# Decayed linear attention and a soft mixture of experts: late weights loaded into nine buffers that attention leaves, four key turns left out, another order of the first loads and of attention's last steps

## The chip, the cores and the metric

One core of a Trainium2 chip. The metric is the device time of one execution in microseconds (us). All data are float32. TensorE (PE) multiplies, VectorE (DVE), ScalarE (ACT) and GpSimd (POOL) do the elementwise work, and every DMA of the program is issued by SyncE (SP), in the order in which the program names them.

## The reference

Attention runs over 4 batches, 8 heads, 768 positions and 64 channels with one decay `lam` for each head. A block's output is its masked scores times its values plus its decayed queries times the state that earlier blocks left:

```python
intra = np.einsum('bhic,bhjc->bhij', qb, kb) * Dmask[None]
intra = np.einsum('bhij,bhjd->bhid', intra, vb)
inter = np.einsum('bhid,bhde->bhie', qb * lam_pow[None], kv_state)
out[:, :, sl] = intra + inter
...
kv_state = lam_block[None, :, None, None] * kv_state + np.einsum('bhsd,bhse->bhde', kb_dec, vb)
```

The result is taken as 3072 tokens `x` of 512 numbers and goes through a soft mixture of 8 experts with 4 slots each: `logits = x @ phi`; a softmax over the tokens gives the inputs of the 32 slots; every expert does `relu(slot @ w1[e]) @ w2[e]` (512 to 1024 to 512); a softmax over the slots mixes their outputs back into every token. `w1` and `w2` have 16.8 MB each, `q`, `k`, `v` and the output 6.3 MB each.

## The kernel before, in words

The sequence is cut into 24 chunks of 128 positions, and the kernel works on twelve pairs `p` of chunks, the same chunk `n` of two batches. Pairs 0 to 5 are chunks 0 to 5 of batches 0 and 1, pairs 6 to 11 those of batches 2 and 3. The instructions of each engine run in program order (`InOrder`, line 36).

**One pair in the loop** (line 410). `carried` multiplies state and scaled queries, `values` adds masked scores times values in the PSUM banks `xb`, ACT copies the result to `XT`, and `state` (not in the last chunk of a batch) multiplies decayed keys and values; DVE adds that to the state. Then PE does the next pair's `scores`, which DVE masks into `at`, and turns: `turn_k` transposes the next pair's keys, of which DVE makes the decayed keys `kd`; `turn_x` transposes this pair's result, and ACT copies it to `X`. `kd` is read by `state` alone, which pairs 5 and 11 do not run, though their keys are turned. Every second pair does `logits`, and `slots` and `gather` add an earlier group to the slots' running sum `acc`.

**The loads.** A pair's `q`, `k` and `v` (512 KB each) are issued two pairs ahead, each kept behind a PE step of the current pair (`next_load`, line 390 and on). `next_weights` issues one 512 KB tile of `w1`, up to three a pair, into the 32 buffers of the pool `slab`; they are full after pair 9. `w2` has 32 tiles of 512 KB (`load_late`). Five go where pairs 10 and 11 no longer load `q`, `k` and `v`, two into `kd` and `qs` after the loop (lines 467, 468), and 25 into slabs, whose `w1` must have been used first by `first(0)` or `first(1)`.

**The start** (lines 129 to 156): `k` of pair 0, the decays `lam`, then `q` and `v`, each as one DMA for both chunks. DVE makes the mask of eight scans once `lam` is there. `turn_k` of pair 0 uses the banks that `values(0)` needs next (line 406).

**After the loop** (lines 470 to 512): the last group's `logits`, `slots` of the group before it, the maxima, `turn_x` of pair 11, four transposes of stored logits, the exponentials `e`, their transpose `d`, two more transposes, the last slot sums, and a transpose on DVE whose result `sT` is what the experts read. Then come `first(0)` and `first(1)` (the `w1` of experts 0 to 3 and 4 to 7), a long elementwise stretch on DVE, ACT and POOL that makes the mixing weights in the layouts `CR` and `ct`, and `second(0)` and `second(1)` (the `w2`). `second(0)` completes the left half of the experts' outputs; twelve outputs of 256 KB (`put`) of this half are given between the products of `second(1)`, and twelve of the right half after it. A bank of `put` is copied by ACT and DVE in turn and sent by SP.

Of the kernel before, what the change touches and what calls it, by code (L numbers as in the profile page):

```python
# [8 lines left out]
F32 = mybir.dt.float32  # L9
F32R = mybir.dt.float32r  # L10
AF = mybir.ActivationFunctionType
ALU = mybir.AluOpType
AX = mybir.AxisListType

P = 128
B, H, S, DH = 4, 8, 768, 64
# [34 lines left out]
def decay_attn_soft_moe(  # L51
# [30 lines left out]
    def chunk(p, x):  # L82
        b, n = PAIR[p]
        return (b + x) * NB + n
# [7 lines left out]
    def load_in(p, which):  # L92
        for x in which:
            tl = loads.tile([P, 2, 512], F32, tag=x, name=x)
            b, n = PAIR[p]
            src = {"q": qT, "k": kT, "v": vN}[x].rearrange("(b n) p c -> n p b c", n=NB)
            go = sp.dma_start(out=tl, in_=src[n, :, b:b + 2])
            IN[x, p] = tl
        return go
# [20 lines left out]
    def load_late(pool_=None, tag="slab", bufs=None):  # L120
        Q, f, i = late.pop()
        kw = {} if bufs is None else {"bufs": bufs}
        t_ = (pool_ or slabs).tile([P, 2, 512], F32, tag=tag, name="w2t", **kw)
        go = sp.dma_start(out=t_, in_=w2[4 * Q + 2 * i:4 * Q + 2 * i + 2, f].rearrange("e p d -> p e d"))
        for y in range(2):
            wt["w2", Q, 2 * i + y, f] = t_[:, y, :]
        return go

    load_in(0, "k")
    sp.dma_start(out=lam_sb, in_=lam)  # L130
    load_in(0, "qv")
    load_in(1, "kqv")
    for a in range(2):
        for hh in range(2):
# [4 lines left out]
    load_early(2)  # L139


    warm = keep.tile([P, 512], F32, tag="x", name="warm", bufs=6)
    dve.memset(warm, 0.0)
    wps = bank("s")
    for _ in range(NWARM):
# [34 lines left out]
                op1=ALU.add,  # L180
            )

    lsum = const.tile([P, 1], F32, name="lsum")
    acc = const.tile([P, D], F32, name="acc")
    e = const.tile([P, P], F32, name="e")
    d = const.tile([P, P], F32, name="d")
# [2 lines left out]

    XT, X = {}, {}  # L190
    run = {}
    at = work.tile([P, 2, 2, HP * P], F32, tag="at", name="at")
    kd = work.tile([P, 2, HP, 2, DH], F32, tag="kd", name="kd")
    qs = work.tile([P, 2, HP, P], F32, tag="qs", name="qs")
    st = work.tile([P, 2, HP, DH], F32, tag="st", name="st")
    dec = work.tile([P, 2, HP, DH], F32, tag="dec", name="dec")
    xb = [bank("a0"), bank("a1")]
    wb = [bank("w0"), bank("w1"), bank("w2"), bank("w3")]
    rb = bank("r")
# [10 lines left out]
    def scores(p):  # L210
        k_, q_ = (IN[x, p].rearrange("p x (a i) -> p x a i", a=HP) for x in "kq")
        first = []
        for x in range(2):
            for hp in range(HP):
                for hh in range(2):
                    mm = pe.matmul(
                        out=wb[2 * x + hh][:, hp * P:hp * P + P],
                        lhsT=k_[rows(hh), x, hp],
                        rhs=q_[rows(hh), x, hp],
                        start=True,  # L220
                        stop=True,
                    )
                    if hp + hh == 0:
                        first.append(mm)
            for hh in range(2):
                dve.tensor_tensor(
                    out=at[:, x, hh], in0=wb[2 * x + hh], in1=mask[:, hh].rearrange("p a i -> p (a i)"), op=ALU.mult
                )
        return first

# [5 lines left out]
    def turn_k(p, x, tk):  # L236
        for hp in range(HP):
            c = slice(hp * P, hp * P + P)
            pe.transpose(tk[:, c], IN["k", p][:, x, c], ident)
        dve.tensor_tensor(  # L240
            out=kd[:, x],
            in0=tk.rearrange("p (a b c) -> p a b c", a=HP, b=2),
            in1=kpow.broadcast_to([P, HP, 2, DH]),
            op=ALU.mult,
        )

    def turn_x(p, x):
        tr = xb[x]
        first = None
        for y in range(HP):  # L250
            mm = pe.transpose(tr[:, y * P:y * P + P], XT[p][:, x, y, :], ident)
            first = first or mm
        xn = keep.tile([P, D], F32, tag="x", name="x", bufs=6)
        act.copy(out=xn, in_=tr)
        X[p, x] = xn
        return first

    def place(x, hh, hp):
# [19 lines left out]
    def values(p):  # L278
        v_ = IN["v", p].rearrange("p x (h c) -> p x h c", h=H)
        first = None  # L280
        for x in range(2):
            for hh in range(2):
                for hp in range(HP):
                    mm = pe.matmul(
                        out=place(x, hh, hp),
                        lhsT=v_[:, x, HP * hh + hp],
                        rhs=at[:, x, hh, hp * P:hp * P + P],
                        start=(PAIR[p][1] == 0 and x == 0 and hp < 2),
                        stop=True,
                        skip_group_check=True,  # L290
                    )
                    first = first or mm
        return first
# [23 lines left out]
        return first  # L317


    sel = const.tile([P, SL], F32, name="sel")  # L320
    gsel = const.tile([P, 4], F32, name="gsel")
    own2 = const.tile([P, 2], F32, name="own2")
    blk = const.tile([P, 4, SL], F32, name="blk")
    blk_ = blk.rearrange("p g s -> p (g s)")
    pl = rb[:, 0:P]
# [44 lines left out]
    def slots(g):  # L370
        first = None
        for c, m in enumerate(members(g)):
            mm = pe.matmul(
                out=wb[2][SL * c:SL * c + SL, :], lhsT=d[:, SL * c:SL * c + SL], rhs=X[m], start=True, stop=True
            )
            first = first or mm
        return first
# [15 lines left out]
    def next_load(p, which, at_):  # L393

        if p + 2 < NP:
            behind(load_in(p + 2, which), at_)
        else:
            behind(load_late(loads, which, 2), at_)

    def next_weights(at_):  # L400
        if early:
            behind(load_early(1), at_)


    scores(0)
    turn_k(0, 0, xb[0])
    turn_k(0, 1, xb[1])
    powers()

    for p in range(NP):  # L410
        b, n = PAIR[p]
        even = p % 2 == 0
        more = p + 1 < NP
        g = (p - 2) // 2 if p >= 2 else None


        m1 = carried(p) if n > 0 else None
        if g is not None and even:
            new = highest(g)
            weigh(g, new)  # L420


        m2 = values(p)
        next_load(p, "k", m1 or m2)
        next_weights(m2)
        if more and PAIR[p + 1][1] > 0:
            scale_q(p + 1)
        XT[p] = keep.tile([P, 2, HP, P], F32, tag="xt", name="xt", bufs=2)
        for hh in range(2):
            act.copy(  # L430
                out=XT[p][:, :, 2 * hh:2 * hh + 2],
                in_=xb[hh].rearrange("p (x a i) -> p x a i", x=2, a=2),
            )
        if g is not None and not even and more:
            gather(g)
        if n < NB - 1:
            m2 = state(p)
        next_load(p, "q", m2)
        if not more:
            break  # L440


        m3, m4 = scores(p + 1)
        next_load(p, "v", m3)
        next_weights(m4)


        if g is not None and even:
            turn_e()
        turn_k(p + 1, 0, wb[0])  # L450
        m5 = turn_x(p, 0)
        next_weights(m5)
        turn_k(p + 1, 1, wb[1])
        turn_x(p, 1)


        if not even:
            logits((p - 1) // 2)
        elif g is not None and p < NP - 2:
            slots(g)  # L460
        if p == 0:
            reduce_selectors()
# [1 line left out]
        load_early(1)  # L464


    load_late(work, "kd")
    load_late(work, "qs")
    g = G - 1
    own = const.tile([P, 1], F32, name="own")  # L470
    gm = const.tile([P, 4], F32, name="gm")
    logits(g)
    slots(g - 1)
    new = highest(g)
    act.copy(out=L[:, g], in_=pl)
    dve.tensor_scalar(out=gm, in0=gsel, scalar1=new, scalar2=None, op0=ALU.mult)
    cm = bank("s")
    pe.matmul(out=cm[:, 0:4], lhsT=blk_, rhs=gm, start=True, stop=True)
    turn_x(NP - 1, 0)
    turn_x(NP - 1, 1)  # L480
    lt = [bank("w0"), bank("w1")]
    for i in range(4):
        pe.transpose(lt[0][:, i * P:i * P + P], L[:, i], ident)
    dve.tensor_reduce(out=own, in_=cm[:, 0:4], axis=AX.X, op=ALU.min)
    gather(g - 1)
    rs = small.tile([P, 1], F32, tag="rs", name="rs")
    act.activation(out=e, in_=pl, func=AF.Exp, bias=own, scale=1.0, accum_out=rs)
    wgt = small.tile([P, 1], F32, tag="alpha", name="alpha")
    act.activation(out=wgt, in_=run["m"], func=AF.Exp, bias=own, scale=-1.0)
    dl = bank("r")  # L490
    pe.transpose(dl[:, 0:P], e, ident)
    for i in range(4, G):
        pe.transpose(lt[1][:, i * P - 512:i * P - 512 + P], L[:, i], ident)
    dve.tensor_copy(out=d, in_=dl[:, 0:P])
    selw = small.tile([P, SL], F32, tag="selw", name="selw", bufs=1)
    dve.tensor_scalar(out=selw, in0=sel, scalar1=wgt, scalar2=None, op0=ALU.mult)

# [83 lines left out]
            quad(d_, Q, f, w, n == 0, n == len(todo) - 1)  # L581

    first(0, denominators)
    for _ in range(4):
        load_late()

# [42 lines left out]
    while late:  # L629
        load_late()  # L630

    so = work.tile([P, D], F32, tag="st", name="so")
    po1 = bank("w0")
    obanks = ("a0", "a1", "s", "w1", "r")
    nput = [0]
# [112 lines left out]
```

## Time and profile before

| | |
|---|---|
| Median of 3 runs | 173.4 us (172.97 to 174.13) |
| The profiled execution | 173.3 us |
| Its span, first to last instruction | 171.5 us |
| Busy: PE, DVE, ACT, POOL | 151.0, 93.9, 54.0, 43.2 us |
| DMA | 59.14 MB, mean 345 GB/s over the span |

The span is what the trace covers; 1.8 us of the profiled execution lie outside it. Times in the rows are counted from the span's start. "Idle before" is how long an engine stood still ahead of an instruction, with what released it; DMA share is the mean busy share of the sixteen DMA engines (it can read a little over 1).

### The profile page before, as it was taken

To read this page: it belongs to the slowest core of one execution; us is meant where nothing else is said; L and a number is where in the kernel's file an instruction comes from. 1 tells how busy PE (TensorE), PEld (TensorE's weight loads), DVE (VectorE), ACT (ScalarE), POOL (GpSimd) and SP (SyncE) were. 2 spreads that over 40 slices of the span, in tenths; PEclk is the share of its full clock that TensorE was granted. 3 is DMA by queue.
4 is the path that set the end of the run, shared out by engine and by line. 5 is a ranking of instruction groups with operands and counts; after the bars stand their busy time and mean duration, and the time that the engine had idled before them with its cause. 6 is when DMAs were issued, how large, how long until landed. Compare 5 with 4: busy or idle time off the path is not lost. (4 is left out here: it accounts for less than half of the span.)

```text
span 171.5 us, 5461 instructions
## 1 busy us (share of the span) xinstructions
PE 151.0 (88%) x2314; PEld 114.7 (67%) x2314; DVE 93.9 (55%) x183; ACT 54.0 (32%) x122; POOL 43.2 (25%) x58
## 2 busy tenths in 40 slices
PE   6869999999999999999999999879999289999500
PEld 6759798979897988899979997543333045447400
DVE  1887473746655579285837472321565893344700
ACT  2012323222432353215232422410124892424500
POOL 1007354343410034345352500000024670000000
PEclk9999999999999999999999999999999969999985
DMA  5999999999999999999999986906999999999995
GB/s 148 394 364 394 400 390 401 379 362 382 363 346 355 293 409 393 398 391 396 385 372 363 372 259 186 346 10 208 343 366 394 385 387 384 387 383 379 372 362 191
DMA packets 30376, 59.14 MB, mean 345 GB/s; under 512 B 2704, under 2 KB 8848, under 8 KB 30352
## 3 DMA queue, kind: packets, MB, share of 16 engines
q1 hardware_dynamic: 30352, 58.80, 94.8%
q8 instruction: 18, 0.29, 0.7%
q14 instruction: 6, 0.05, 0.1%
HBM read 52.50 MB, written 6.29 MB: 343 GB/s over the span
## 5 line engine op out<-in xcount | busy, mean ns | idle before, releaser
L45 POOL TENSOR_TENSOR qs<-q,qpow 128x512 f32<-128x512 f32 x20 | 25.0, 1271 | 55.3 <-DMA q<-qT 29.2
L45 DVE TENSOR_TENSOR at<-w,mask 128x512 f32<-128x512 f32 x48 | 29.8, 683 | 6.5 <-PE w L45 6.5
L45 PE MATMUL w<-q,k 64*128 64x128 f32 x384 | 24.7, 278 | 0.5 <-DMA q<-qT 0.5
L45 PE MATMUL a<-at,v 128*64 128x128 f32 x384 | 23.8, 276 | 1.3 <-DVE kd L45 1.3
L45 PEld LDWEIGHTS w<-q,k 64*128 64x128 f32 x384 | 22.4, 188 | 1.6 <-issue 0.9
L45 PEld LDWEIGHTS a<-at,v 128*64 128x64 f32 x384 | 20.7, 137 | 3.7 <-DVE kd L45 1.8
L45 ACT COPY x<-a 128x512 f32<-128x512 f32 x24 | 14.0, 586 | 26.2 <-PE a L45 26.2
L45 ACT COPY xt<-a 128x512 f32<-128x512 f32 x24 | 12.9, 589 | 28.3 <-PE a L45 28.2
L45 DVE TENSOR_TENSOR st<-dec,s 128x512 f32<-128x512 f32 x8 | 5.5, 688 | 21.3 <-PE s L45 20.0
L45 PE MATMUL a<-ident,xt 128*128 128x128 f32 x96 | 14.3, 273 | 0.0
L45 PE MATMUL r<-w2t,hz 128*32 128x256 f32 (+1 forms) x128 | 10.7, 497 | 4.0 <-DVE hz L45 4.0
L45 DVE TENSOR_TENSOR kd<-w,mask 128x512 f32<-128x512 f32 x22 | 14.1, 681 | 0.0
L45 PE MATMUL w<-ident,k 128*128 128x128 f32 x88 | 13.5, 277 | 0.0
L45 PEld LDWEIGHTS a<-qs,st 64*64 64x64 f32 x320 | 9.0, 132 | 5.6 <-issue 4.5
L45 PE MATMUL a<-qs,st 64*64 64x128 f32 x320 | 11.9, 276 | 0.6 <-ACT x L45 0.6
L45 PEld LDWEIGHTS r<-w2t,hz 128*32 128x32 f32 x128 | 4.7, 126 | 10.2 <-DVE hz L45 4.5
L45 PEld LDWEIGHTS a<-ident,xt 128*128 128x128 f32 x96 | 11.2, 141 | 0.0
L45 PE MATMUL s<-v,kd 128*64 128x64 f32 x320 | 11.0, 222 | 0.0
L45 PEld LDWEIGHTS s<-v,kd 128*64 128x64 f32 x320 | 10.7, 138 | 0.0
L45 PEld LDWEIGHTS w<-ident,k 128*128 128x128 f32 x88 | 10.0, 141 | 0.7
L45 POOL TENSOR_TENSOR dec<-st,qpow 128x512 f32<-128x512 f32 x8 | 8.5, 1057 | 5.6 <-DVE st L45 5.5
L45 POOL TENSOR_TENSOR CN<-CN,cmx 128x512 f32<-128x512 f32 (+1 forms) x2 | 1.7, 832 | 29.5 <-DVE cmx L45 29.5
(112 smaller groups left out, 171.0 us busy)
## 6 DMA issues: line engine op xcount, KB each, us to landing
w1t<-w_x SPq DMA_DIRECT2D x32, 512.0 KB, 6.4
w2t<-w_x SPq DMA_DIRECT2D x32, 512.0 KB, 7.6
k<-kT SPq DMA_DIRECT2D x12, 512.0 KB, 5.9
q<-qT SPq DMA_DIRECT2D x12, 512.0 KB, 6.2
v<-vN SPq DMA_DIRECT2D x12, 512.0 KB, 6.5
y<-o SPq DMA_DIRECT2D x24, 256.0 KB, 4.4
phi_sb<-phi_x SPq DMA_DIRECT2D x4, 16.0 KB, 7.1
lam_sb<-lam_x SPq DMA_DIRECT2D x1, 6.0 KB, 3.6
```

The source lines that it names most:

```text
L45: return self._tc.keep_in_program_order(f(*args, **kwargs))
```

## The change

`kd` and `turn_k` are left out for pairs 5 and 11. At the start `lam` is loaded first, then `k` and `q` of pair 0 chunk by chunk in four DMAs of 256 KB, then `v` as before; `turn_k` of pair 0 uses two other banks. `at` is split into two tiles, one per chunk, `st` and `dec` become halves of one tile `sd`, and three tiles of `X` hold both chunks of a pair in place of six that hold one. Sixteen of the 32 `w2` tiles, where it was seven, go into buffers that attention leaves: `kd` (now in pair 10), `mask` (in pair 11), `qs`, `sd`, `at1`, `v` and `xt` after the loop, two of `x` after the last slot sums' inputs are ready, and one more `x` and `at0` behind `first(0)`. Twelve `w2` tiles instead of 21 are left for the slabs behind `first(1)`. After the loop `turn_x` of pair 11 comes ahead of `slots`, all six transposes of logits follow the transpose of `e`, and ACT instead of DVE copies `d`; the second half of the last `XT` is copied by DVE.

```diff
-    load_in(0, "k")
     sp.dma_start(out=lam_sb, in_=lam)
-    load_in(0, "qv")
+    for which in "kq":
+        IN[which, 0] = loads.tile([P, 2, 512], F32, tag=which, name=which)
+    for x in range(2):
+        sp.dma_start(out=IN["k", 0][:, x], in_=kT[chunk(0, x)])
+        sp.dma_start(out=IN["q", 0][:, x], in_=qT[chunk(0, x)])
+    load_in(0, "v")
     load_in(1, "kqv")
...
-    turn_k(0, 0, xb[0])
-    turn_k(0, 1, xb[1])
+    turn_k(0, 0, rb)
+    turn_k(0, 1, sb)
...
         next_load(p, "k", m1 or m2)
+        if p == NP - 1:
+            load_late(work, "mask")
...
-            act.copy(
+            copy = act.copy if more or hh == 0 else dve.tensor_copy
+            copy(
...
         next_load(p, "q", m2)
+        if p == NP - 2:
+            load_late(work, "kd")
...
-        turn_k(p + 1, 0, wb[0])
+        turns = PAIR[p + 1][1] < NB - 1
+        if turns:
+            turn_k(p + 1, 0, wb[0])
         m5 = turn_x(p, 0)
         next_weights(m5)
-        turn_k(p + 1, 1, wb[1])
+        if turns:
+            turn_k(p + 1, 1, wb[1])
         turn_x(p, 1)
...
-    load_late(work, "kd")
-    load_late(work, "qs")
+    for tag in ("qs", "sd", "at1"):
+        load_late(work, tag)
+    load_late(loads, "v", 2)
+    load_late(keep, "xt", 2)
...
     logits(g)
-    slots(g - 1)
     new = highest(g)
     act.copy(out=L[:, g], in_=pl)
+    turn_x(NP - 1, 0)
+    turn_x(NP - 1, 1)
     dve.tensor_scalar(out=gm, in0=gsel, scalar1=new, scalar2=None, op0=ALU.mult)
     cm = bank("s")
     pe.matmul(out=cm[:, 0:4], lhsT=blk_, rhs=gm, start=True, stop=True)
-    turn_x(NP - 1, 0)
-    turn_x(NP - 1, 1)
+    slots(g - 1)
+    dve.tensor_reduce(out=own, in_=cm[:, 0:4], axis=AX.X, op=ALU.min)
     lt = [bank("w0"), bank("w1")]
-    for i in range(4):
-        pe.transpose(lt[0][:, i * P:i * P + P], L[:, i], ident)
-    dve.tensor_reduce(out=own, in_=cm[:, 0:4], axis=AX.X, op=ALU.min)
-    gather(g - 1)
...
     pe.transpose(dl[:, 0:P], e, ident)
-    for i in range(4, G):
-        pe.transpose(lt[1][:, i * P - 512:i * P - 512 + P], L[:, i], ident)
-    dve.tensor_copy(out=d, in_=dl[:, 0:P])
+    for i in range(G):
+        pe.transpose(lt[i // 4][:, i % 4 * P:i % 4 * P + P], L[:, i], ident)
+    gather(g - 1)
+    act.copy(out=d, in_=dl[:, 0:P])
+    for _ in range(2):
+        load_late(keep, "x", 3)
...
     first(0, denominators)
+    load_late(keep, "x", 3)
+    load_late(work, "at0")
     for _ in range(4):
         load_late()
```

## Rows read from the trace of the kernel before

**Rows 1.** The windows view of five stretches: the engines' busy time, clock, DMA share, GB/s.

```profile
core 0: us, PE busy (x) PEld busy (x) DVE busy (x) ACT busy (x) POOL busy (x), PEclk, DMA share, GB/s
30.00:60.00 30.00, 30.00 (x527) 26.24 (x524) 18.13 (x31) 9.30 (x21) 7.62 (x7) 1.00 0.99 354
60.00:98.00 38.00, 38.00 (x721) 33.44 (x721) 24.72 (x41) 12.51 (x32) 15.97 (x14) 1.00 1.02 387
98.00:122.00 24.00, 22.26 (x320) 14.05 (x320) 7.29 (x20) 6.16 (x14) 0.73 (x1) 1.00 0.66 212
122.00:154.30 32.30, 28.00 (x300) 12.02 (x292) 20.75 (x45) 14.71 (x35) 8.76 (x22) 0.95 1.05 385
154.30:169.50 15.20, 6.44 (x44) 4.83 (x44) 5.22 (x9) 4.38 (x8) 0.00 (x0) 0.88 1.06 366
```

**Rows 2.** The chain of waits, last long piece: start us, us, what.

```profile
143.45 10.88 DMA w2t<-w_x
```

**Rows 3.** PE's own waits over the span: in total, times, longest us.

```profile
PE r L45 <- DVE hz L45: 4.0, 1, 4.0
PE a L45 <- DVE kd L45: 1.3, 1, 1.3
PE a L45 <- ACT x L45: 0.6, 2, 0.3
```

**Rows 4.** The timeline of the first pair: start us, us, engine, operation, idle before.

```profile
4.91 2.63 DVE L45 TENSOR_TENSOR_SCAN mask<-lam_sb,ident 128x128 f32<-128x128 f32 x8 [3.51 <-DMA lam_sb<-lam_x]
6.15 2.06 PE L45 MATMUL w<-q,k 64*128 64x128 f32 x32 [0.54 <-DMA q<-qT]
...
7.46 2.46 DVE L45 TENSOR_TENSOR at<-w,mask 128x512 f32<-128x512 f32 x4
...
9.83 1.28 DVE L45 TENSOR_TENSOR kd<-a,mask 128x512 f32<-128x512 f32 x2
...
10.57 2.13 PE L45 MATMUL a<-at,v 128*64 128x128 f32 x32 [1.34 <-DVE kd L45]
...
12.53 1.10 PE L45 MATMUL s<-v,kd 128*64 128x64 f32 x32
```

**Rows 5.** The timeline where pair 11's keys are turned.

```profile
101.41 0.60 PE L45 MATMUL w<-ident,k 128*128 128x128 f32 x4
...
101.84 0.60 PE L45 MATMUL a<-ident,xt 128*128 128x128 f32 x4
...
103.36 0.58 ACT L45 COPY x<-a 128x512 f32<-128x512 f32 x1 [0.29 <-PE a L45]
...
103.99 1.10 PE L45 MATMUL a<-qs,st 64*64 64x128 f32 x30 [0.32 <-ACT x L45]
```

**Rows 6.** The timeline of attention's end.

```profile
108.24 1.03 PE L45 MATMUL w<-x,d 128*32 128x512 f32 x7
...
110.33 1.08 ACT L45 COPY x<-a 128x512 f32<-128x512 f32 x2 [1.19 <-PE a L45]
...
111.30 0.37 ACT L45 ACTIVATE e<-r,own 128x128 f32<-128x128 f32 x1
...
114.27 3.64 PE L45 MATMUL a<-w1t,e 128*32 128x512 f32 x32 [0.44 <-DVE e L45]
```

**Rows 7.** The timeline of the experts' second products and of the first right-half output.

```profile
137.84 5.35 PE L45 MATMUL r<-w2t,hz 128*32 128x256 f32 x64 [4.02 <-DVE hz L45]
...
154.38 1.06 PE L45 MATMUL w<-w2t,hz 128*32 128x256 f32 x12 [0.36 <-DMA w2t<-w_x]
...
157.69 0.59 ACT L45 COPY o<-s 128x512 f32<-128x512 f32 x1 [0.62 <-DVE s L45]
```

**Rows 8.** DMA issues begun at 103.7 us and at 166.4 and 167.2 us: KB, us to landing.

```profile
w2t<-w_x SPq DMA_DIRECT2D x1, 512.0 KB, 4.0
...
y<-o SPq DMA_DIRECT2D x2, 256.0 KB, 3.5
```

**Rows 9.** The windows view of the slice behind PE's wait and the next one.

```profile
137.20:141.49 4.29, 3.65 (x44) 1.90 (x48) 4.17 (x10) 4.15 (x12) 3.39 (x9) 0.66 1.05 389
141.49:145.78 4.29, 4.29 (x57) 2.27 (x50) 1.65 (x5) 1.14 (x3) 0.00 (x0) 0.95 1.05 383
```

More of the change, by code (lines that the diff above doesn't have):

```diff
@@ L139, in decay_attn_soft_moe @@
     load_early(2)
-    warm = keep.tile([P, 512], F32, tag="x", name="warm", bufs=6)
+    warm = keep.tile([P, 512], F32, tag="x", name="warm", bufs=3)
     dve.memset(warm, 0.0)
@@ L181, in powers @@
             )
-    lsum = const.tile([P, 1], F32, name="lsum")
+    lsum = head.tile([P, 1], F32, name="lsum")
     acc = const.tile([P, D], F32, name="acc")
@@ L191, in decay_attn_soft_moe @@
     run = {}
-    at = work.tile([P, 2, 2, HP * P], F32, tag="at", name="at")
+    at = [work.tile([P, 2, HP * P], F32, tag=f"at{x}", name="at") for x in range(2)]
     kd = work.tile([P, 2, HP, 2, DH], F32, tag="kd", name="kd")
     qs = work.tile([P, 2, HP, P], F32, tag="qs", name="qs")
-    st = work.tile([P, 2, HP, DH], F32, tag="st", name="st")
-    dec = work.tile([P, 2, HP, DH], F32, tag="dec", name="dec")
+    sd = work.tile([P, 2, 2, HP, DH], F32, tag="sd", name="sd")
+    st, dec = sd[:, 0], sd[:, 1]
     xb = [bank("a0"), bank("a1")]
@@ L226, in scores @@
                 dve.tensor_tensor(
-                    out=at[:, x, hh], in0=wb[2 * x + hh], in1=mask[:, hh].rearrange("p a i -> p (a i)"), op=ALU.mult
+                    out=at[x][:, hh], in0=wb[2 * x + hh], in1=mask[:, hh].rearrange("p a i -> p (a i)"), op=ALU.mult
                 )
@@ L252, in turn_x @@
             first = first or mm
-        xn = keep.tile([P, D], F32, tag="x", name="x", bufs=6)
-        act.copy(out=xn, in_=tr)
-        X[p, x] = xn
+        if x == 0:
+            last = p == NP - 1
+            run["x"] = (
+                work.tile([P, 2, D], F32, tag="at0", name="x") if last
+                else keep.tile([P, 2, D], F32, tag="x", name="x", bufs=3)
+            )
+        X[p, x] = run["x"][:, x]
+        act.copy(out=X[p, x], in_=tr)
         return first
@@ L286, in values @@
                         lhsT=v_[:, x, HP * hh + hp],
-                        rhs=at[:, x, hh, hp * P:hp * P + P],
+                        rhs=at[x][:, hh, hp * P:hp * P + P],
                         start=(PAIR[p][1] == 0 and x == 0 and hp < 2),
@@ L317, in state @@
         return first
-    sel = const.tile([P, SL], F32, name="sel")
-    gsel = const.tile([P, 4], F32, name="gsel")
-    own2 = const.tile([P, 2], F32, name="own2")
+    sel = head.tile([P, SL], F32, name="sel")
+    gsel = head.tile([P, 4], F32, name="gsel")
+    own2 = head.tile([P, 2], F32, name="own2")
     blk = const.tile([P, 4, SL], F32, name="blk")
@@ L464, in decay_attn_soft_moe @@
         load_early(1)
-    load_late(work, "kd")
-    load_late(work, "qs")
+    for tag in ("qs", "sd", "at1"):
+        load_late(work, tag)
+    load_late(loads, "v", 2)
+    load_late(keep, "xt", 2)
     g = G - 1
-    own = const.tile([P, 1], F32, name="own")
-    gm = const.tile([P, 4], F32, name="gm")
+    own = head.tile([P, 1], F32, name="own")
+    gm = head.tile([P, 4], F32, name="gm")
     logits(g)
-    slots(g - 1)
     new = highest(g)
     act.copy(out=L[:, g], in_=pl)
+    turn_x(NP - 1, 0)
+    turn_x(NP - 1, 1)
     dve.tensor_scalar(out=gm, in0=gsel, scalar1=new, scalar2=None, op0=ALU.mult)
@@ L630, in decay_attn_soft_moe @@
         load_late()
-    so = work.tile([P, D], F32, tag="st", name="so")
+    so = work.tile([P, D], F32, tag="qpow", name="so")
     po1 = bank("w0")
```

## The prediction

> **What bounds the kernel now.** I read the windows view first, because the busy table misleads here: PE is 88% busy over the span, yet it does not set the end. From 122 us on the DMA engines are full (share 1.05 and 385 GB/s to 154.3 us, then 1.06) until almost the end of the span [rows 1]. The chain of waits says the same: its last long piece is a `w2` tile that lands 10.9 us after its issue, behind other tiles, at 154.3 us [rows 2], and then the outputs drain at 366 GB/s, 0.262 MB / 366 GB/s = 0.72 us each [rows 1]. Ahead of that there is a hole: from 98 to 122 us only 212 GB/s move [rows 1]. At the later rate 24.0 us x (385 - 212) = 4.15 MB more would have gone through, 10.8 us of DMA. Before the hole PE leads: from 30 to 98 us it is busy throughout, in the loop it waits for nothing but 0.6 us on ACT [rows 1, 3], and the DMA, at 354 GB/s from 30 to 60 us, has some room. So attention is a PE chain, the tail is a DMA chain, and between them the DMA has nothing it may load because the buffers are taken.
>
> **The late weights.** Nine more tiles go into attention's buffers, 9 x 0.524 = 4.72 MB, which is more than the 4.15 MB of the hole. I placed each by its last reader: `kd` is free behind pair 10's `state`, `mask` behind pair 11's masking, `qs` and `sd` behind `carried(11)`, `at1` and `v` behind `values(11)`, `xt` behind the last `logits`, the `x` behind `slots` and the last sums. SP issues in this order and each of these ends later than the one before, so no load stands long ahead of a ready one. A tile takes 0.524 MB / 385 GB/s = 1.36 us, and sixteen tiles between about 93 and 110 us are 22 us of work, so DMA no longer runs dry before the slabs come free. The last `w2` tile then lands near 154.3 - 10.8 - 2.7 (attention being shorter, below) - 1.9 (of the outputs 0.7 MB already moved before 154.3: 24 x 0.262 = 6.29 MB less 15.2 us x 366 GB/s) = 139 us. DMA alone would end the span at about 171.5 - 10.8 - 2.7 = 158.0. It does not set the end any more, because the outputs cannot start so early. What is late next is the compute chain, which I follow now.
>
> **The start, -1.85 us.** Now the masks wait for `lam` until 4.91, `at` starts behind the masks at 7.46, `kd` follows to 11.1, and PE stands 1.34 us before `values(0)` since `turn_k` occupies its banks [rows 4]. With `lam` issued first, half a microsecond earlier, the masks start at 4.4 or a little before; with the chunk loads, scores of chunk 0 start near 5.65, when PE's warm-up products are through. DVE: 4.4 + 2.63 + 2.46 + 1.28 = 10.8 for the last `kd`. `values(0)` has its own banks and follows the transposes at 8.6, so `state(0)` starts with the last `kd`, at 10.7 against 12.53 [rows 4]: 1.85 gained. It is handed on, as PE is the chain from there. The two extra issues on SP delay the later loads by 1.0 us at most, behind transfers already queued. Bounds: 0.5 (the earlier `lam` only) to 2.1.
>
> Here a rule speaks against the change. The Trainium skill, "DMA: Bandwidth & Descriptors", section "Anatomy of one DMA", gives every DMA a fixed cost of about 2.0 us beside its bytes at 436 GB/s; paid one after the other, four loads of 256 KB would take an estimated 4 x 2.6 = 10.4 us and the sum would lose what the start gains. The rows have outputs of the same size draining at 366 GB/s, 0.72 us apiece [rows 1], so in a full queue the fixed part overlaps, and I leave the sum at -1.85.
>
> **The key turns, -1.60 us.** Each `turn_k` holds PE 101.84 - 101.41 = 0.43 us [rows 5], two a pair. Pair 5's two give 0.86: `slots` follows there, which hides ACT's copies. At pair 11 the next step, `carried(11)`, needs both copies of `x`; they end at 103.94 [rows 5] and move by 0.74 when the turns go, as ACT's two copies of 0.58 then follow each other. Sum 1.60; bounds 0.8 (ACT's copies set it both times) and 1.7. The four `kd` on DVE are off the chain.
>
> **Attention's end, -0.95 us.** Now `e` waits for the `x` copies that end at about 111.3 because `turn_x` comes behind `slots` (over at 109.3) [rows 6]. With `turn_x` first, its copies run beside `slots`. I walked it with the same durations: `slots` ends 1.2 later than now, `e` starts 0.9 earlier, the transposes of logits fit between `e`'s transpose and ACT's copy of `d`, and `gather` is done 0.2 before `d`. `first(0)` starts 0.95 earlier. Bounds 0 (`gather`'s new place, in front of `selw` and the bank that the last sums need, eats it) to 1.5. The `XT` copy moved to DVE starts earlier but is 0.15 longer: nothing.
>
> **The stretch from `first(0)` to the second products, 0.** PE waits 4.02 us for `hz` [rows 3, 7], which hangs on DVE and ACT work that follows `first(0)`; the change touches none of it. It moves as a whole by 1.85 + 1.60 + 0.95 = 4.4 us.
>
> **`second(1)`, -1.05 us.** All its tiles are there, so the wait before 154.38 goes: the last product follows the earlier ones at once, 1.05 earlier by PE's pace between them. The first copy of the right half ends not at 157.69 + 0.59 = 158.28 [rows 7] but at 158.28 - 4.4 - 1.05 = 152.8.
>
> **The sum.** The left half's twelve outputs have drained by then to within two. The right half: issue 152.9; landing of the first 3.0 us later (a tile of twice the size, alone in the queue, took 4.0 [rows 8]; less half of its data, 0.7, and a little less as the queue is moving; bounds 2.3 and 3.5); eleven more at 0.72 = 7.9; and 0.9 from the last landing (167.2 + 3.4 now [rows 8]) to the end of the span. 152.9 + 3.0 + 7.9 + 0.9 = 164.7, against 171.5: -6.8. The profiled execution's 173.3 becomes 166.5; the median of the runs shown is 0.1 above it, which I ignore. The unknown costs put the forecast's own range at 164.2 (all upper gains, outputs at 0.68) to 168.2 (start 0.5, key turns 0.8, end 0.3).
>
> **The rivals.**
> *The PE chain gains only from the tail* (chance 0.12): the earlier start is eaten by loads of pairs 2 and 3, which the full DMA cannot bring sooner, and the key turns by ACT. Then only 0.95 + 1.05 stand: 158.28 - 2.0 + 0.1 + 3.0 + 7.9 + 0.9 = 168.2, 170.0 us. For it: q of pair 2 has little slack; against: PE's empty list of waits on loads [rows 3].
> *The hole stays* (0.07), the case in which the change doesn't do what it says: a buffer is handed out whose last reader is later than I think, SP stands in front of it, and the rest queues behind. DMA then still ends the kernel and moves only with the slabs: 173.3 - 4.4 = 168.9. SP's order, above, is against it.
> *DMA stays the bound and the compute chain shrinks more* (0.06): were the elementwise stretch shorter as well, the end would approach 158.0, 159.8 us; 162.5 is half way. Nothing in the change shortens that stretch.
> *Each small load pays its fixed cost* (0.02): the first scores would come about 5 us later, 171.5 us.
> *Slower* (0.03): PE's clock does not come back. Behind PE's 4.02 us of idling the granted clock is 0.66 in the slice from 137.2 and 0.95 in the next [rows 9], so it fell to the lower of its two levels (1.2 of 2.4 GHz) and returned under steady work. In the new kernel the same idle stretch comes before `second(1)`, which is then chopped by outputs. If the clock stayed down, the rest of `second(0)` would take 1.9 more, the twelve product groups of `second(1)` 5.0, the outputs' products and spreads between them 4.9: 166.5 + 11.8 = 178.3. It decides against the change from three quarters of that on, so only if the clock stays low through nearly all of `second(1)`. The Trainium skill, "TensorE: Matmul & The Clock Gate", section "HAM oscillation — how this bites in real kernels", warns of such re-throttling with every wait; the trace has it once, and recovered.
>
> **How the numbers follow.** The forecast has 0.65; 0.05 is left for no gain at all (hole kept, earlier PE work lost), 172 to 174. The range, 8 in 10: the low end 164.0 leaves out most of the fast rival, the high end 170.0 takes in the forecast, the kept hole and the short PE gain. About 1% is what a measurement of this kernel can tell from no change, so faster means under 171.7: 0.65 + 0.12 + 0.07 + 0.06 + 0.01 = 0.91; same 0.06; slower 0.03.
>
> **What would show it.** Right: 370 GB/s or more from 95 to 120 us; the last `w2` landing near 139 us; `first(0)` starting at 109.9; the idle 4 us before `second(0)`'s last part still there, now near 129.5 to 133.5; DMA idle for some microseconds around 140; outputs from 142.6. Wrong: DMA still below 300 GB/s after 98 us, `first(0)` later than 111.5, or PE waits for `q` or `k` in pairs 2 to 4.

## The result: 166.8 us, and where the time went

| | before | after |
|---|---|---|
| Median of the runs | 173.64 us | 166.82 us (165.62 to 167.54) |
| Profiled execution, its span | 173.3, 171.5 us | 167.54, 165.8 us |

The ratio is 0.960 (95% interval 0.953 to 0.968). The forecast was 166.5 us, in a range of 164.0 to 170.0. Single runs over 1.5% longer than the fastest of their kernel are left out of the ratios and of what is read from profiles below, though not of the medians.

The windows view of the changed kernel answers to [rows 1]; its stretches follow the same stages, and the columns are the same.

```profile
30.00:60.00 30.00, 29.96 (x534) 25.87 (x532) 18.30 (x32) 9.14 (x20) 7.38 (x8) 1.00 1.03 389
60.00:95.00 35.00, 35.00 (x659) 30.81 (x657) 21.77 (x37) 11.93 (x30) 14.93 (x13) 1.00 1.02 379
95.00:119.00 24.00, 23.18 (x338) 14.44 (x338) 7.66 (x20) 5.82 (x14) 1.71 (x2) 1.00 1.00 360
119.00:139.00 20.00, 15.98 (x172) 5.89 (x167) 15.93 (x38) 11.04 (x28) 8.81 (x22) 0.86 1.05 407
139.00:150.00 11.00, 11.00 (x118) 5.43 (x110) 3.45 (x6) 3.38 (x7) 0.00 (x0) 0.95 0.52 184
```

The hole is gone: 360 GB/s stand in the 24 us where it was 212 [rows 1]. It comes back at another place, from 139 to 150 us, where DMA is half idle (0.52) because no output is ready. The chain of waits had a `w2` tile as its last long piece before [rows 2]. Now its end runs through elementwise copies into `ct`, through `h` and `hz` on DVE (the hidden values of experts 4 to 7 and their transpose, which the last part of `second(0)` reads), and through PE (start us, us, what):

```profile
121.56 9.36 DMA w2t<-w_x
...
132.27 0.42 DVE ct L45
132.69 0.03 issue
132.73 0.75 DVE h L45
133.48 0.01 issue
133.49 0.72 DVE hz L45
134.21 0.04 issue
134.26 6.57 PE r L45 x64
```

The view puts a `w2` tile that lands at 130.92 ahead of the copies. That landing did not release them, as DVE's copies into `ct` (casts to fp32r, a second 32-bit type, in which the kernel keeps `ct`) begin at 130.69 (timeline below). So the view says that the bound has moved from the DMA to the compute chain, and the experiments test it. The timeline after, for the steps of [rows 4 to 7]:

```profile
2.57 2.63 DVE L45 TENSOR_TENSOR_SCAN mask<-lam_sb,ident 128x128 f32<-128x128 f32 x8 [1.17 <-DMA lam_sb<-lam_x]
...
5.59 2.76 PE L45 MATMUL w<-q,k 64*128 64x128 f32 x32
...
7.49 2.48 DVE L45 TENSOR_TENSOR at<-w,mask 128x512 f32<-128x512 f32 x4 [2.29 <-PE w L45]
...
11.22 1.15 PE L45 MATMUL s<-v,kd 128*64 128x64 f32 x32
...
101.14 0.85 PEld L45 LDWEIGHTS a<-qs,sd 64*64 64x64 f32 x30 [0.28 <-ACT x L45]
...
107.27 0.37 ACT L45 ACTIVATE e<-r,own 128x128 f32<-128x128 f32 x1
...
110.69 3.64 PE L45 MATMUL a<-w1t,e 128*32 128x512 f32 x32 [0.43 <-DVE e L45]
...
130.69 2.01 DVE L45 CAST ct<-part 32x256 fp32r<-32x256 f32 x5
...
134.26 6.57 PE L45 MATMUL r<-w2t,hz 128*32 128x256 f32 x64 [4.02 <-DVE hz L45]
...
150.60 1.50 PE L45 MATMUL w<-w2t,hz 128*32 128x256 f32 x24
...
154.38 0.59 ACT L45 COPY o<-s 128x512 f32<-128x512 f32 x1 [0.62 <-DVE s L45]
```

Read against the rows before, each step is earlier by: `state(0)` 12.53 - 11.22 = 1.31; `carried(11)` 103.99 - 101.14 = 2.85 (its products behind ACT's copy; after, the row of their weight loads); `first(0)` 114.27 - 110.69 = 3.58; the last part of `second(0)` 137.84 - 134.26 = 3.58; the first right-half copy 157.69 - 154.38 = 3.31.

### The profile page after: what moved, and what is told of

Read it like the earlier page. It is cut to its first block, busy times and chain, and to the rows that moved or that the text cites. A ratio compares the mean times of both kernels' runs of the same rounds, so it can differ in the third digit from the quotient of the medians.

```text
span 165.8 us, 5417 instructions
## 1 busy us (share of the span) xinstructions
PE 150.9 (91%) x2298; PEld 113.8 (69%) x2298; DVE 91.3 (55%) x179; ACT 53.7 (32%) x122; POOL 43.3 (26%) x58
## 4 chain that ended last, share of the span: by engine, by line
PE 83%; DMA 6%; DVE 4%; issue 1%; ACT 1%; DVEq 0%
PE a L45 33%; PE w L45 31%; PE r L45 10%; PE s L45 9%; DMA w2t<-w_x 6%; DVE o L45 1%; DVE ct L45 1%; DVE h L45 0%; DVE acc L45 0%; DVE hz L45 0%; DVEq L766 0%; ACT x L45 0%; DVE warm L45 0%; DVE s L45 0%; ACT s L45 0%
## 5 line engine op out<-in xcount | busy, mean ns | idle before, releaser
L45 PE MATMUL w<-q,k 64*128 64x128 f32 x384 | 25.4, 283 | 0.0
L45 PEld LDWEIGHTS w<-q,k 64*128 64x128 f32 x384 | 23.1, 193 | 1.1 <-issue 0.4
L45 DVE TENSOR_TENSOR sd<-sd,s 128x512 f32<-128x512 f32 x8 | 5.5, 688 | 21.3 <-PE s L45 20.0
L45 PE MATMUL r<-w2t,hz 128*32 128x256 f32 (+1 forms) x128 | 11.9, 542 | 4.0 <-DVE hz L45 4.0
L45 PEld LDWEIGHTS a<-qs,sd 64*64 64x64 f32 x320 | 9.0, 132 | 5.7 <-issue 4.6
L45 PEld LDWEIGHTS r<-w2t,hz 128*32 128x32 f32 x128 | 5.0, 140 | 11.2 <-issue 5.3
L45 PE MATMUL a<-qs,sd 64*64 64x128 f32 x320 | 11.9, 276 | 0.6 <-ACT x L45 0.3
L45 DVE TENSOR_TENSOR kd<-w,mask 128x512 f32<-128x512 f32 x18 | 11.5, 681 | 0.0
L45 PE MATMUL w<-ident,k 128*128 128x128 f32 x72 | 11.1, 277 | 0.0
L45 POOL TENSOR_TENSOR sd<-sd,qpow 128x512 f32<-128x512 f32 x8 | 8.5, 1061 | 5.7 <-DVE sd L45 5.7
L45 PEld LDWEIGHTS w<-ident,k 128*128 128x128 f32 x72 | 8.1, 140 | 0.7
## 6 DMA issues: line engine op xcount, KB each, us to landing
w2t<-w_x SPq DMA_DIRECT2D x32, 512.0 KB, 10.2
```

The lines of the kernel that those rows point to most:

```text
L45: return self._tc.keep_in_program_order(f(*args, **kwargs))
```

## The experiments

All ratios are against the kernel before, run on the same chip.

**Weights only.** The nine late tiles, with start, turns and last steps as before:

```diff
-    for tag in ("qs", "sd", "at1"):
+    for tag in ("kd", "qs", "sd", "at1"):
...  (first loads, key turns and attention's end as in the kernel before)
```

> Only the nine late tiles of the change (kd behind the loop); start, key turns and attention's end as before. Theory A (the hole of the DMA was the bound; once it is filled the compute chain ends the kernel): the chain keeps its place but for the wait before the last w2 products, so the first right-half copy ends at 158.3 - 1.0 = 157.3 and the span at 157.3 + 10.8 (as in the changed kernel) = 168.1: 169.9 us. Rival B (the earlier PE work made the gain, the DMA would have caught up anyway): no change, 173.5 us.

Measured: 169.62 us, 0.975 (0.971 to 0.980). Theory A was met within 0.3 us, rival B fell: the loads alone bring 4 us, and no PE work had to be saved for it. From 142 us on PE works throughout and the DMA is busy for 0.64 of the time, so it is the compute chain that ends this kernel:

```profile
142.00:158.00 16.00, 15.94 (x162) 9.18 (x151) 6.93 (x13) 6.11 (x12) 0.00 (x0) 1.00 0.64 226
```

**All but the weights.**

```diff
-        if p == NP - 1:
-            load_late(work, "mask")
...
-    load_late(keep, "x", 3)
-    load_late(work, "at0")
```

> The changed kernel without the nine late tiles (seven go into attention's buffers, as before). Theory A: the hole is back and the DMA chain ends the kernel; it moves only as slabs come free earlier, 3.6 us: 173.5 - 3.6 = 169.9 us, with the last w2 landing near 150.7 and outputs queued behind it. Rival B: the gain stays, 166.8 us.

Measured: 168.51 us, 0.970 (0.966 to 0.973), between the two. A second set of runs of the same kernel gave the profile:

> The changed kernel without the nine late tiles again, for a profile of an undisturbed run (168.5 us): DMA near 200 GB/s or less between attention's end and the middle of first(0), the last w2 landing near 149 and the outputs queued behind it.

Measured: 167.61 us, 0.965 (0.960 to 0.970). Its windows view:

```profile
95.00:119.00 24.00, 23.20 (x332) 13.88 (x330) 8.04 (x20) 5.81 (x14) 0.89 (x1) 1.00 0.71 239
119.00:148.00 29.00, 24.98 (x274) 10.87 (x264) 18.63 (x42) 14.52 (x35) 8.81 (x22) 0.94 1.05 401
148.00:164.00 16.00, 7.40 (x62) 5.42 (x58) 5.97 (x11) 4.58 (x9) 0.00 (x0) 0.81 1.02 357
```

The hole is back (239 GB/s, where 200 or less was expected) and DMA is full from 119 to 164 us, as theory A has it. What it missed is the rate: 401 GB/s for the `w2` stream, not the 385 of [rows 1]. The gains do not add: 4.0 for the weights and 5.1 for the rest make 9.1, the two together 6.8. Each alone runs into the other bound. On top of the other steps the nine tiles are worth only 1.3 to 1.7 us (166.36 us, below, against 167.61, and 166.82 against 168.51), and as the intervals overlap that size is rough.

**The second profile of the kernel before**, to see whose rate that is.

> The kernel before, for a second profile. Its profile on record moves w2 at 385 GB/s behind 122 us, those of the changed kernel and of most variants at 400 to 405. If that belongs to the kernel before, this profile has 385 GB/s again and 173.5 us, and 2 us of the gain come from a faster stream (25 tiles at 1.354 - 1.275 us); if it differs from run to run of one kernel, it has about 400 GB/s here and a span near 169.5.

Measured: 173.28 us, ratio 1.000 (0.996 to 1.004), and in its profile:

```profile
98.00:122.00 24.00, 22.26 (x324) 14.22 (x322) 7.20 (x19) 6.16 (x14) 0.90 (x1) 1.00 0.61 220
122.00:154.30 32.30, 28.08 (x304) 11.85 (x300) 20.87 (x45) 14.71 (x35) 8.76 (x22) 0.95 1.04 379
```

It is 385 and 379 GB/s in the kernel before, and 400 to 407 in the changed kernel and the variants that share its tiles. Over 25 tiles this is about 25 x (0.524 MB / 382 - 0.524 MB / 403 GB/s) = 1.8 us of DMA time. It counts where the DMA is the bound, as in the kernel without the late tiles; the end of the changed kernel is set by the compute chain. Why the stream is faster is open: the variants differ from the kernel before in their tiles' places, in what is in flight and in the issue times, and none of these was tried by itself.

**Clock.** Four products whose result nobody reads fill PE's wait for `hz`:

```diff
+        for _ in range(4):
+            pe.matmul(out=idle, lhsT=ident, rhs=L[:, 0:4].rearrange("p a b -> p (a b)"), start=True, stop=True)
...
-    second(0, po, {})
+    second(0, po, {8: busy})
```

> The changed kernel with four extra 128x512 products (result unused) in PE's wait for hz. Theory D (the lower clock behind that wait costs time): the clock stays at its upper level, the 16 product groups take 0.21 instead of 0.43 each, outputs start 1.6 (3.4 us at the lower level) to 2.9 us (6.8 us) earlier: 164.0 to 165.3 us and less spread. Rival: the clock is not what holds the outputs, 166.8 us, or 0.3 more for the extra products.

Measured: 164.36 us (164.14 to 165.27), 0.948 (0.945 to 0.951). The windows view over the 64 products behind the wait, first of the changed kernel:

```profile
134.26:140.66 6.40, 6.40 (x65) 3.01 (x69) 4.35 (x11) 3.93 (x10) 2.83 (x8) 0.54 0.95 365
```

then of this kernel:

```profile
133.79:137.26 3.47, 3.47 (x64) 2.10 (x68) 3.36 (x8) 3.38 (x9) 2.80 (x8) 1.00 1.06 410
```

and of the kernel before:

```profile
137.84:143.00 5.16, 5.16 (x64) 2.76 (x68) 4.32 (x11) 3.93 (x10) 2.79 (x8) 0.67 1.05 386
```

The same products take 3.47 us at a granted clock of 1.00, 5.16 at a mean of 0.67 and 6.40 at 0.54: after the idle 4 us the clock stands at its lower level and returns at different times. Theory D holds. The 6.40 belongs to this one execution of the changed kernel; its second profile (below) has 5.17.

**The other terms one by one**, each undone on top of the kernel with the four products (164.36 us), where runs differ least.

```diff
+    load_in(0, "k")
     sp.dma_start(out=lam_sb, in_=lam)
...  (the chunk loads of k and q, and v, left out)
+    load_in(0, "qv")
...
+    turn_k(0, 0, xb[0])
+    turn_k(0, 1, xb[1])
```

> The changed kernel with the four extra products (164.4 us, little spread), and the first loads and banks as before. If the start is handed on by the PE chain (theory A), state of pair 0 starts near 12.5 instead of 10.8 to 11.2 and all later steps are late by the same 1.3 to 1.7: 165.7 to 166.1 us. Rival (loads of pairs 2 and 3 eat it): 164.4 us.

Measured: 165.87 us, 0.954 (0.951 to 0.957): the start is worth 1.5 us, and it is handed on: `first(0)` follows `state(0)` by 99.41 us here and by 99.44 in the kernel it is compared with.

```diff
-        turns = PAIR[p + 1][1] < NB - 1
+        turns = True
...  (kd is loaded behind the loop)
```

> The changed kernel with the four extra products, and the key turns of pairs 5 and 11 done (kd is then loaded behind the loop). Theory A: first(0) starts 1.6 later than with them left out: 166.0 us. Rival (ACT's copies set the step both times): 0.8 or less, under 165.2 us.

Measured: 165.88 us, 0.956 (0.953 to 0.959): 1.5 us; from `state(0)` to `first(0)` its trace has 1.62 more than the kernel it is compared with.

```diff
-    turn_x(NP - 1, 0)
-    turn_x(NP - 1, 1)
...
+    slots(g - 1)
...  (the old order down to the copy of d)
```

> The changed kernel with the four extra products, and attention's last steps in the order of before. The two traces put the gain of the new order at 114.27 - 105.02 = 9.25 less 110.69 - 102.17 = 8.52, 0.73 from values(11) to first(0), against 0.95 predicted: 165.1 us. Rival: gather's new place eats it, 164.4 us.

Measured: 165.24 us, 0.951 (0.948 to 0.954): 0.9 us, and 0.75 in the same stretch of its trace. The interval overlaps that of the kernel with the four products (0.945 to 0.951), so it is the trace that carries this size.

**What the compute chain is made of.** `first(1)`, with its `h` and `hz`, is moved ahead of the copies into `CR` and `ct`:

```diff
     dve.transpose(out=parts[1], in_=CN)
+    first(1)
     act.copy(out=parts[0].bitcast(F32R), in_=parts[1])
...
-    first(1)
```

> The changed kernel with the activation and transposes of experts 4 to 7 (hz) put ahead of the copies that make CR and ct. If the compute chain ends the changed kernel (theory A), PE's 4 us wait goes, second(0) is done near 134 instead of 140.7, outputs start near 137, and the DMA becomes the bound again: w2 until 142.2, then 24 outputs at 0.69, end of span near 160: 161.8 us. Rival C (outputs are held by the DMA in the changed kernel too): no change, 166.8 us.

Measured: 166.95 us, 0.962 (0.958 to 0.966), no gain over 166.82: my expectation failed. Its timeline shows why:

```profile
133.31 1.05 PE L45 MATMUL w<-w2t,hz 128*32 128x256 f32 x16
138.20 0.37 ACT L45 COPY so<-r 128x256 f32<-128x256 f32 x1
138.62 1.22 PE L45 MATMUL w<-so,blk 128*128 128x256 f32 x2 [4.27 <-ACT so L45]
```

`second(0)` is done at 133.3, 7 us earlier, but ACT copies `so` (its result, out of PSUM) at 138.20, behind its share of the 48 copies into `ct`. PE's wait only changed its place, from `hz` to `so`, and its clock fell there instead (0.50 from 138.62 to 141.50 us). This points at the copies as the chain; the next two runs test that.

```diff
-    stack((act.copy, pool.tensor_copy, dve.tensor_copy))   (three times)
+    stack((act.copy, dve.tensor_copy))
+    stack((pool.tensor_copy,))   (twice)
```

> The changed kernel with hz put first (as in the run that gained nothing), and the 48 copies into ct shared out otherwise: the first 16 by ACT and DVE, the other 32 by POOL alone. If the elementwise copies ahead of the experts' sums (so) are what holds the first output (theory A2: ACT and DVE busy with ct until 138.2), so is copied near 134.5, outputs start near 138, w2 lands until 142.2 as now, and the outputs drain behind it: 142.2 + 24 x 0.68 + 1.1 = 159.6, 161.4 us; the DMA is the bound again. If something else holds the outputs, 166.9 us as before that.

Measured: 164.48 us, 0.948 (0.944 to 0.952). The first half of the expectation held (outputs from 138.08), the second did not, as POOL was too slow for the last sixteen. The rows are of the slowest of the six runs (166.5 us):

```profile
138.08 11.27 SPq L45 DMA_DIRECT2D y<-o  x10
...
145.68 0.80 PE L45 MATMUL w<-s,ct 128*128 128x256 f32 x2 [2.77 <-POOL ct L45]
```

With half of those given to ACT and DVE between the first outputs:

```diff
-    stack((pool.tensor_copy,))
+    stack((pool.tensor_copy, None))   (None: kept, and copied one by ACT and one by DVE with each put)
```

> As the run before it, but half of the last 16 copies into ct is done by ACT and DVE between the first outputs, so that POOL is done near 142.5 instead of 145.6 and the ninth output does not wait for it (2.77 us). Theory A2 (elementwise copies hold the outputs; without them the DMA is the bound again): outputs from 138, no PE wait, right-half copies from about 148.4, w2 in by 142.2 to 143.7, 24 outputs at 0.68 behind it and 1.1: span 159.6 to 161.1, 161.4 to 162.9 us. Rival (outputs are held elsewhere too): 164.5 us.

Measured: 161.87 us, 0.930 (0.926 to 0.934), within the expectation and faster than both kernels. Its windows view:

```profile
119.00:142.00 23.00, 23.00 (x270) 10.30 (x262) 17.37 (x40) 11.73 (x28) 12.38 (x31) 1.00 1.05 403
142.00:158.00 16.00, 7.92 (x68) 5.58 (x66) 6.56 (x11) 4.94 (x9) 0.00 (x0) 0.84 0.99 348
```

From 119 us to its last product PE never waits and its clock stays at 1.00 (the 0.84 takes in PE's idle time behind its last product), and DMA is full until the span's last 1.6 us: the DMA is the bound again, now without a hole. So it was the copies that held the outputs.

**The changed kernel again.**

> The changed kernel once more, beside the others on one chip: 166.8 us; if the clock behind PE's wait varies from run to run, runs with the lower share of granted clock are about 1.5 us slower than those with the higher one.

Measured: 166.36 us, 0.958 (0.953 to 0.962). The second part of the expectation is borne out only in part. In the first set of runs the two with a share of 0.964 took 167.4 and 167.5 and the two with 0.974 took 165.6 and 166.3, some 1.5 us less; in this set shares of 0.962 to 0.964 took 166.1, 166.2 and 167.3, and 0.972 and 0.973 took 166.5 and 165.5. The share over the whole span also counts the idle end, so it does not tell what the clock cost. The window behind the wait does; in the profiled execution (166.5 us, span 164.7) it reads:

```profile
134.43:139.60 5.17, 5.17 (x65) 2.81 (x69) 4.37 (x11) 3.93 (x10) 2.84 (x8) 0.67 1.05 406
```

The wait is the same 4.02 us, and the products behind it take 5.17 us. Of six profiles with this wait, over the two kernels and their variants, five have 5.0 to 5.2 us and one the 6.40. So the clock's return varies from one execution of the same kernel to the next.

## Why the prediction was right, step by step

- **The bound and its change.** Right: DMA with a hole before, the compute chain after, shown by the two single halves and by the last kernel. Of the signs that were named, the idle 4 us came as foreseen (130.24 to 134.26) and DMA is half idle behind 139 us; 360 GB/s in the old hole fell short of 370, `first(0)` started at 110.69, not 109.9, and the outputs at 144.6, not 142.6. The last `w2` tile lands at 142.2 (issued at 131.85, 10.3 later), not 139; which part of that sum was off was not taken apart.
- **The start, -1.85.** 1.31 in the two profiles shown, 1.5 in the times. All profiles together are nearer to the forecast: `state(0)` starts at 10.2 to 11.2 us in nine with the new start (10.8 in mean, 10.7 was forecast) and at 12.2 to 12.8 in four with the old one. The mechanism was off: `lam` came at 2.5, not 4.4 (1.7 us after its issue with nothing ahead, 3.6 before), so the masks were early and DVE waited 2.29 us for PE's scores. In the profile shown these took 2.76 us, against 2.06 before, at a granted clock of 1.00 both times; why is open. The rival that loads eat the start came true in small: in two of the nine profiles, one of them the second of the changed kernel, PE waited 0.60 us for `q` of pair 2, which was also named as a sign of being wrong.
- **Small loads.** The rival that each small load pays its fixed cost did not come true: the chunk loads, issued within 1.4 us of each other, landed 3.1 and 3.5 us after issue (median of two). The section of the Trainium skill that the prediction names, "Anatomy of one DMA" in "DMA: Bandwidth & Descriptors", gives its 2.0 us for DMAs that GpSimd issues; here SyncE issues them, so it did not speak of these loads.
- **Key turns, -1.60.** 2.85 - 1.31 = 1.54 in the profile, 1.5 in the times. Right.
- **Attention's end, -0.95.** 3.58 - 2.85 = 0.73; 0.9 in the times. Right in kind, a little less in size.
- **The elementwise stretch, 0.** 23.57 us from `first(0)` to the last part of `second(0)`, before and after. Right. Its successor was taken as unchanged: the products behind the wait took 6.40 us in this execution instead of 5.16, 1.24 us, as the clock came back later. The second profile of the changed kernel has 5.17, so this is a difference between executions and not shown to be a cost of the change. The prediction had a clock that stays down as a rival for the whole of `second(1)`; it happened in small, in one of the two profiles.
- **`second(1)`, -1.05.** 12.44 us from 143.00 to 155.44 before, 11.45 from 140.66 to 152.11 after: 0.99. Right.
- **The outputs.** First right-half copy at 155.0 against 152.8, late by the sum of the above, of which the clock is the largest part; from there 10.8 us to the end against 11.9, as the drain was faster (eleven landings in 7.5 us, not 7.9, and the first 2.2 after its issue, not 3.0). So 2.1 us too early and 1.1 too long leave 165.8 against 164.7 for the span. In the second profile the copy is done at 153.9, and 1.1 too early and 1.1 too long give 164.7 exactly.
- **Two sums that do not come out.** The forecast's own range of 164.2 to 168.2 does not follow from its bounds: the upper gains and 0.68 an output give 165.2 (164.5 with the first landing at its lower bound), and a start of 0.5, key turns of 0.8 and an end of 0.3 give 166.5 + 1.35 + 0.8 + 0.65 = 169.3. And half way between 159.8 and 166.5 lies 163.2, not 162.5. The measured time lies inside either range.

The good agreement thus rests partly on luck, two errors of opposite sign: the first output comes later than forecast, and the drain behind it is shorter. Of the rivals, "DMA stays the bound and the compute chain shrinks more" is what the 161.87 us kernel made true by another change.

## What to carry to other kernels

Fill a hole in a DMA-bound kernel, but follow the compute chain to the first output as well: what the hole was worth is cut off there, and two changes that each meet the other's bound do not add. When a wait is removed and nothing moves, read what ended the new wait; here it was the same elementwise copies, one consumer later. A PE wait costs its length and then what the next products lose at the lower clock, here 1.7 to 2.9 us behind 4.02. And one profile is one execution: a start that gained 1.31 us in one pair of profiles gained 1.7 in the mean of all, and the late return of the clock was gone in the second profile.

## What the runs showed of the hardware

- Behind an idle stretch of 4.02 us on PE, 64 products took 5.16 us in the kernel before and 6.40 and 5.17 in two executions of the changed one, by the clock granted; with four products of no use (3.7 us) in the wait they took 3.47 at a granted clock of 1.00, and the kernel 2.0 to 2.5 us less.
- A load of 6 KB that was first in the queue landed in 1.7 us, behind one load of 512 KB in 3.6 us.
- The same `w2` loads streamed at 379 and 385 GB/s in two profiles of the kernel before and at 400 to 407 in the changed one and most variants; the cause is open.
